# A gated linear attention followed by an MLP mixer: the mixer input of batch 0 made transposed in PSUM, channel weights loaded in three-chunk pieces, all orders rewritten

## The chip, the cores and the metric

The kernel runs on one core of a Trainium2 chip. The metric is the device time in microseconds (us) of one execution; shorter is better. Five engines work side by side and meet at semaphores: TensorE (PE: matrix products into PSUM), VectorE (DVE), ScalarE (ACT), GpSimd (POOL) and SyncE (SP, which issues most of the DMA transfers). Each engine takes its instructions strictly in the order in which the program lists them, apart from weight loads (PEld), which run ahead of the products.

## The reference

For each of 4 batches, 8 heads and 768 positions a 48x48 state is decayed, updated and read; the eight heads' outputs side by side make a row `x` of 384 values per position, and these go through a token mixer and a channel mixer:

```python
for t in range(S):                                  # S = 768
    state = alpha[:, :, t, :, None] * state + k[:, :, t, :, None] * v[:, :, t, None, :]
    y[:, :, t] = einsum('bhd,bhde->bhe', q[:, :, t], state)
x = y.transpose(0, 2, 1, 3).reshape(4, 768, 384)
h  = relu(x.transpose(0, 2, 1) @ w_tok1) @ w_tok2   # w_tok1 768x256, w_tok2 256x768
u  = x + h.transpose(0, 2, 1)
out = u + relu(u @ w_ch1) @ w_ch2                   # w_ch1 384x1536, w_ch2 1536x384
```

Inputs and output are float32 in HBM; the products are made in bfloat16.

## The kernel before, in words

The attention is worked in 12 chunks `n` = 0 to 11, three per batch, each of 256 positions held as 128 partitions by 2 slots. Every chunk has four loads of 384 KB (`ld_at` alpha, `ld_kt` k, `ld_qt` q, `ld_vt` v). ACT takes logarithms (`ln`), PE sums them along the positions with a triangular matrix (`cum`), ACT makes the decay factors (`E`, `IE`), DVE or POOL multiply them into q and k (`qq`, `kk`, line 700), both are transposed (`trq`, `trk` on PE at line 712 and `evq`, `evk` out of PSUM; for `n` from 6 on by DMA, `dq`, `dk`, line 725), PE makes the position-by-position products (`G`) that DVE masks (`mask`, line 770), PE makes the state update (`K`), DVE adds and scales it (`sa`, `sm`, `s`), and PE makes the output from the masked products (`y`) and from the state before (`ia`, `ib`). `x` copies it out of PSUM. Many small products share the helper of line 643.

The mixer of batch `b` follows. `t1` (line 878) and the relu `ht` are the first token product. `t2` (line 883) is the second, one 128-position tile `i` at a time, with its result laid out positions by channels; `u` (line 887, DVE) adds `x`. The channel product needs `u` transposed. For batches 1 to 3 a DMA does that (`ux`, line 729, one for each half of the positions); for batch 0 PE transposes (`up`, line 894, 18 products of 128 columns in three groups) and `ut` copies the result out of PSUM. `c1` (line 902, 24 blocks of three 384-column products per batch) and the relu `rt` (lines 873 and 875, on ACT or DVE) are the first channel product; `c2` (line 907, four blocks per tile) and `o` (line 911, DVE, which adds `u`) the second; `st` stores (line 624).

The weights come through the same 19 input buffers as the attention inputs: `ldw` loads a piece of 384 KB, `cw` casts it to bfloat16. `wc1` (w_ch1) has six pieces, each one 128-row chunk by 768 columns, so that the first `c1` block waits for three pieces; `wt2` has two pieces of 128 rows.

Nothing is scheduled when the kernel runs. A planner was run beforehand, and its answer is written into the file: `ORDER` lists all operations with a letter for the engine (`t` PE, `s` ACT, `v` DVE, `g` POOL, `y` SP), and each engine follows it; `BUFS` says which buffer each value takes. `f8_cumw1` and the like are filler products on zeros ahead of an operation on PE: the number counts units, three of which make one float32 product (line 643, `128*64 128x384 f32`) and the rest bfloat16 products of 512 columns.

Of the kernel before, what the change touches and what calls it, by code (L numbers as in the profile page):

```python
# [56 lines left out]
def either(*ds):  # L57
    out = {}
    for d in ds:
        out.update(d)  # L60
    return out
# [40 lines left out]
UP = (0,)  # L102
# [18 lines left out]
def build(g):  # L121

    P = Plan()
# [6 lines left out]
    def fillers():  # L130
        for o in list(P.ops):
            nm = o.name
            if "PE" in o.eng and (nm[:4] in ("t1_0", "t2_0", "up_0") or nm.split("_")[-1][-1] in "0123" and nm[:2] not in ("t1", "t2", "up", "c1", "c2") and not nm.endswith("10") and not nm.endswith("11")):
# [182 lines left out]
    def mixer(b):  # L316
# [15 lines left out]
        us = []  # L332
        for i in range(NS):
            if i % 3 == 0:
                u = V("u")
            bank = V("one")
            o = P.op(f"t2_{b}_{i}", pe([384] * 2), m0 + (1900 + 330 * i) * sc, writes=[bank],
                     reads=[h for h, _ in hts], preds=[h for _, h in hts] + [wl[("wt2", p)] for p in range(2)],
                     emit=lambda e, i=i, bank=bank: g.tok2(bank, i, [h for h, _ in hts]))
            uo = P.op(f"u_{b}_{i}", dve(384), m0 + (1950 + 330 * i) * sc, writes=[u], reads=[bank, x[i][0]], preds=[o],  # L340
                      emit=lambda e, i=i, bank=bank, u=u: g.uadd(u, i, bank, x[i][0]))
            us.append((u, uo))
        ut = V("ut")
        uts = []
        if b in UP:
            for p in range(3):
                bank = V("one")
                o = P.op(f"up_{b}_{p}", pe([128] * 6), m0 + (3900 + 340 * p) * sc, writes=[bank],
                         reads=list(dict.fromkeys([us[2 * p][0], us[2 * p + 1][0]])),
                         preds=[us[2 * p][1], us[2 * p + 1][1]],  # L350
                         emit=lambda e, p=p, bank=bank: g.utr(bank, [us[2 * p][0], us[2 * p + 1][0]], p))
                uts.append(P.op(f"ut_{b}_{p}", either(dve(768, True), act(768)), m0 + (3950 + 340 * p) * sc, writes=[ut],
                                reads=[bank], preds=[o], emit=lambda e, p=p, bank=bank: g.utev(e, ut, bank, p)))
        else:
# [18 lines left out]
        for i in range(NS):  # L373
            hold = 4000.0 if (i >= NS - 3 and b < B - 1) else 0.0
            cuts = [(0, HD // 2), (HD // 2, HD)] if (b, i) == LAST else [(0, HD)]
            for ci, (ca, cz) in enumerate(cuts):
# [33 lines left out]
ld_at1y ld_at0y ln1s ln0s f8_cumw1t f1_cumw1t cumw1t IE1s cumw0t IE0s ld_vt0y E0s vb0g vs0_0g vs1_0v ld_kt0y kk0v  # L410
f8_trk0t f1_trk0t trk0t E1s ld_qt0y qq0v ka0s kb0s kc0v f1_trq0t trq0t ld_kt1y kk1v K0t evq0s s0_0v ld_vt1y vb1s
f1_trk1t trk1t ld_at2y evk0v ln2s f2_G0_0t G0_0t ld_qt1y ka1g sa1_0v f4_cumw2t cumw2t mask0_0v vs0_1s kb1g kc1g vs1_1s
K1t sm1_0g qq1v sa0_1v sm0_1v G1_0t ld_kt2y IE2s E2s trq1t evq1s ib0t mask1_0v f3_y1_0t y1_0t y0_0t evk1v G0_1t sa1_1v
ld_qt2y x1_0s mask0_1v G1_1t ld_vt2y x0_0s vb2s kk2g trk2t kc2s ldw_wt10y qq2g cw_wt10s f2_ia1t ia1t mask1_1v evk2s
trq2t ld_at3y vs1_2g ldw_wt11y evq2v ib1t y1_1t y0_1t vs0_2g ldw_wt21y sm1_1g P3g K2t sa0_2v sm0_2g x0_1s t1_0_0_0t
f1_G0_2t G0_2t ldw_wt20y G1_2t cw_wt20g t1_0_1_0t mask0_2v x1_1s t1_0_1_1t ld_at4y ld_kt3y t1_0_1_2t lnP3s cum3t
cw_wt11s IE3s ia2t y0_2t x0_2s t1_0_0_1t t1_0_0_2t E3s t1_0_0_3t mask1_2v t1_0_1_3t ib2t y1_2t ldw_wc14y t1_0_1_4t
x1_2s t1_0_0_4t f1_t1_0_1_5t t1_0_1_5t ht_0_1v P4g cw_wt21s t1_0_0_5t ht_0_0s f3_t2_0_0t t2_0_0t t2_0_1t u_0_0v ln13s
r13s ldw_wc13y t2_0_2t u_0_1v t2_0_3t u_0_2v t2_0_5t lnP4s t2_0_4t u_0_3v u_0_5v u_0_4v up_0_0t cw_wc14s cw_wc13s
ldw_wc15y up_0_1t ld_qt3y k0a3g kk3g cum4t trk3t cw_wc15g ut_0_0v up_0_2t ut_0_2v ut_0_1s c1_0_11_0t c1_0_8_0t IE4s  # L420
c1_0_11_1t rt_0_8_0v rt_0_11_0v ldw_wc11y q0r3g qq3g c1_0_9_1t rt_0_9_1v ln14s kb3s c1_0_10_0t cw_wc11s c1_0_9_0t
rt_0_9_0v rt_0_11_1v E4s c1_0_7_0t c1_0_10_1t c1_0_7_1t ldw_wc10y r14s cw_wc10s rt_0_10_1v trq3t evk3s rt_0_7_0v
ldw_wc12y ld_vt3y cw_wc12g c1_0_2_0t c1_0_0_1t ka3g rt_0_7_1s c1_0_8_1t rt_0_10_0v vb3v vs1_3g vs0_3g rt_0_0_1v
rt_0_2_0v evq3s ld_at5y ld_qt4y c1_0_1_1t rt_0_8_1v c1_0_3_0t kc3s K3t P5g c1_0_4_1t rt_0_3_0s rt_0_1_1s q0r4g G0_3t
ld_kt4y qq4g s0_3v ln15s G1_3t sa1_3v c1_0_2_1t rt_0_2_1s mask0_3v lnP5s c1_0_1_0t c1_0_5_1t rt_0_5_1s rt_0_1_0s r15s
mask1_3v ldw_wc21y cw_wc21s k0a4g ldw_wc20y c1_0_6_1t rt_0_6_1v c1_0_4_0t kk4v ldw_wc22y c1_0_5_0t c1_0_0_0t cw_wc22s
rt_0_4_0v rt_0_0_0v cw_wc20g rt_0_4_1s c1_0_6_0t rt_0_6_0v c1_0_3_1t trq4t rt_0_3_1v cum5t trk4t ld_kt5y k0a5g
ldw_wc23y rt_0_5_0s c2_0_3_0t c2_0_5_0t evq4s kb4s evk4v ld_qt5y G1_4t mask1_4v G0_4t ld_vt4y c2_0_0_0t IE5s c2_0_0_1t
ka4g cw_wc23s c2_0_3_1t kc4s sm1_3g E5s mask0_4v ib3t y1_3t ldw_wc24y cw_wc24s c2_0_5_1t vb4g vs1_4s x1_3s ia4t
ldw_wc25y vs0_4g cw_wc25s ld_at6y y0_3t kk5v c2_0_3_2t y0_4t q0r5v trk5t evk5s qq5v K4t c2_0_0_2t sa0_4v c2_0_0_3t P6v  # L430
x0_3s ld_at7y sm0_4g o_0_0v trq5t x0_4s sa1_4v P7g evq5s lnP6s c2_0_5_2t c2_0_5_3t ld_vt5y vb5g c2_0_4_0t c2_0_4_1t
ld_kt7y kc5g G1_5t G0_5t lnP7s o_0_5v ib4t y1_4t vs1_5s mask1_5v t1_1_1_0t t1_1_1_1t sm1_4g x1_4s c2_0_4_2t c2_0_3_3t
vs0_5s ld_at8y t1_1_1_2t st_0_5s K5t mask0_5v sa0_5v sm0_5v cum6t t1_1_0_0t ld_kt6y k0a6g t1_1_0_1t ld_qt6y c2_0_2_0t
ln17s ld_qt7y ia5t y0_5t x0_5s IE6s kk6g ib5t y1_5t ln16s E6s t1_1_0_2t x1_5v t1_1_0_3t t1_1_1_3t cum7t E7s o_0_3v
t1_1_1_4t t1_1_1_5t r16s ld_kt8y q0r6g ld_vt6y dk6y P8g ht_1_1v lnP8s t1_1_0_4t t1_1_0_5t c2_0_2_1t c2_0_2_2t ln18s
ht_1_0v t2_1_1t u_1_1v t2_1_2t t2_1_0t t2_1_4t u_1_2v u_1_0v ux_1_0y c2_0_1_0t c2_0_1_1t vb6s IE7s qq6v r17s t2_1_3t
# [529 lines left out]
```

## Time and profile before

| | before |
|---|---|
| time, median of 3 runs (lowest to highest) | 163.17 us (162.33 to 164.11) |
| span of the profiled execution | 160.5 us |
| median less span (launch and end, outside the span) | 2.67 us |
| PE busy | 154.6 us |
| DVE busy | 114.9 us |
| ACT busy | 97.8 us |
| POOL busy | 80.8 us |
| HBM read and written | 25.17 MB and 4.72 MB |

The profile is one execution. Its busy PE is modelled: products overlap one another, so that the distance from one start to the next, not the length of one, says how long a product keeps PE.

### The profile page before, as it was taken

The page shows a single profiled execution, that of the slowest core. Times are in us where ns is not written, and L with a number is a line of the kernel's source. Part 1 is how long each engine was busy: PE and PEld are TensorE (multiplying, and loading weights), DVE is VectorE, ACT ScalarE, POOL GpSimd, SP SyncE. Part 2 cuts the span into 40 slices and gives each one's busy share as a digit, 9 for nine tenths or more (in the row PEclk, how much of TensorE's full clock was granted, in tenths as well). Part 3 has the DMA queues.
Part 4 walks back from the last instruction along what each step waited for, and adds up shares of the span by engine and source line. Part 5 has one row for each costly group of instructions (what it writes and reads, how often), then busy time and mean ns, then how long its engine had stood idle before and what let it go on. Part 6 is the DMA issues. An engine that isn't in the chain of part 4 may idle for free.

```text
span 160.5 us, 3971 instructions
## 1 busy us (share of the span) xinstructions
PE 154.6 (96%) x1563; PEld 97.1 (60%) x1563; DVE 114.9 (72%) x206; ACT 97.8 (61%) x179; POOL 80.8 (50%) x94
## 2 busy tenths in 40 slices
PE   7999989999999999999999999999999999999992
PEld 2545565766667676666667666566567665665661
DVE  6099994979889787989969758795886762464222
ACT  3789999998899955897563583269832203343000
POOL 5205897695973649389778852699523000000000
PEclk9999999999999999999999999999999999999999
DMA  4999999999999999999989999989701235111133
GB/s 122 320 324 317 317 374 311 339 333 306 316 347 324 275 278 272 210 228 319 241 202 298 239 315 204 217 196 134 196 21 62 87 79 169 49 49 53 49 129 116
DMA packets 76130, 35.05 MB, mean 218 GB/s; under 512 B 70352, under 2 KB 74320, under 8 KB 76112
## 3 DMA queue, kind: packets, MB, share of 16 engines
q1 hardware_dynamic: 73808, 31.76, 74.1%
q10 hardware_dynamic: 2304, 3.05, 5.3%
q8 instruction: 12, 0.20, 0.5%
q14 instruction: 6, 0.05, 0.1%
HBM read 25.17 MB, written 4.72 MB: 186 GB/s over the span
## 4 chain that ended last, share of the span: by engine, by line
PE 61%; DMA 12%; DVE 6%; ACT 6%; SPq 6%; POOL 4%; issue 3%; DVEq 0%; POOLq 0%
PE ps L907 22%; PE ps L902 21%; PE ps L643 11%; DMA in<-in_v_dram 6%; SPq L584 6%; DMA out_dram<-o 4%; PE ps L878 3%; PE ps L883 2%; DMA ut<-u 2%; DVE pkk L700 2%; DVE gtm L770 1%; PE ps L712 1%; DVE rt L875 1%; POOL vb L746 1%; POOL pkq L700 1%
## 5 line engine op out<-in xcount | busy, mean ns | idle before, releaser
L907 PE MATMUL ps<-wc,rt 128*128 128x384 bf16 (+1 forms) x300 | 52.4, 319 | 0.0
L902 PE MATMUL ps<-ut,wc 128*128 128x384 bf16 x288 | 50.3, 326 | 0.1
L902 PEld LDWEIGHTS <-wc 128*128 128x128 bf16 x288 | 27.1, 98 | 17.9 <-DMA ut<-u 0.6
L907 PEld LDWEIGHTS <-rt 128*128 128x128 bf16 x300 | 27.8, 98 | 16.0
L873 ACT ACTIVATE rt<-ps 128x384 bf16<-128x384 f32 x47 | 21.4, 492 | 23.6 <-PE ps L902 23.3
L875 DVE TENSOR_SCALAR rt<-ps 128x384 bf16<-128x384 f32 x49 | 25.6, 551 | 9.1 <-PE ps L902 8.9
L770 DVE TENSOR_TENSOR gtm<-ps,mk 128x1024 bf16<-128x1024 f32 x24 | 28.5, 1218 | 3.1 <-PE ps L643 2.8
L911 DVE TENSOR_TENSOR o<-ps,u 128x384 f32<-128x384 f32 (+1 forms) x25 | 13.2, 536 | 12.6 <-PE ps L907 10.1
L700 POOL TENSOR_TENSOR pkk<-in,IE 128x768 bf16<-128x768 f32 x8 | 14.5, 1817 | 3.3 <-DVE ss L844 2.3
L745 ACT CAST x<-ps 128x384 bf16<-128x384 f32 x20 | 9.2, 479 | 11.1 <-PE ps L643 9.5
L887 DVE TENSOR_TENSOR u<-ps,x 128x384 bf16<-128x384 f32 x24 | 12.0, 550 | 3.1 <-PE ps L883 2.5
L746 POOL CAST vb<-in 64x384 bf16<-64x384 f32 (+1 forms) x14 | 8.3, 594 | 10.4 <-DMA in<-in_v_dram 4.7
L692 POOL TENSOR_TENSOR in<-in,in 128x384 f32<-128x384 f32 x8 | 8.0, 1000 | 10.5 <-DVE u L887 3.8
L643 PE MATMUL ps<-rt 128*128 128x512 bf16 (+1 forms) x29 | 12.1, 515 | 1.1 <-DVE rt L541 1.1
L745 ACT CAST vb<-in 64x384 bf16<-64x384 f32 (+1 forms) x18 | 11.4, 634 | 0.8 <-DMA in<-in_v_dram 0.3
L700 POOL TENSOR_TENSOR pkq<-in,E 128x768 bf16<-128x768 f32 x6 | 10.9, 1818 | 0.6 <-DMA tpk<-pkq 0.3
L878 PE MATMUL ps<-x,wt 128*128 128x384 bf16 x48 | 11.0, 325 | 0.0
L844 POOL TENSOR_TENSOR ss<-tmp,E 128x384 bf16<-128x384 f32 x10 | 8.3, 833 | 4.2 <-DVE in L628 3.9
L841 DVE TENSOR_TENSOR tmp<-ps,ss 128x384 f32<-128x384 f32 x16 | 8.8, 552 | 1.8 <-PE ps L643 0.6
L883 PE MATMUL ps<-ht,wt 128*128 128x384 bf16 x48 | 9.1, 326 | 0.0
L643 PE MATMUL ps<-vb,gtm 128*128 128x48 bf16 x192 | 8.2, 183 | 0.2 <-DVE gtm L770 0.2
L643 PE MATMUL ps<-tpq,tpk 48*64 48x128 bf16 (+1 forms) x288 | 7.9, 218 | 0.4 <-POOL tpq L746 0.3
(94 smaller groups left out, 207.6 us busy)
## 6 DMA issues: line engine op xcount, KB each, us to landing
in<-in_alpha_dram SPq DMA_DIRECT2D x12, 384.0 KB, 5.1
in<-in_v_dram SPq DMA_DIRECT2D x12, 384.0 KB, 5.6
in<-in_k_dram SPq DMA_DIRECT2D x12, 384.0 KB, 5.2
in<-in_q_dram SPq DMA_DIRECT2D x12, 384.0 KB, 5.5
in<-in_moe_w_ch_dram SPq DMA_DIRECT2D x12, 384.0 KB, 5.9
out_dram<-o ACTq DMA_DIRECT2D x15, 192.0 KB, 1.8
in<-in_moe_w_tok_dram SPq DMA_DIRECT2D x4, 384.0 KB, 6.0
out_dram<-o SPq DMA_DIRECT2D x8, 192.0 KB, 2.2
```

The source lines that it names most:

```text
L643: return self.pe.matmul(out, lhsT=lhsT, rhs=rhs, start=start, stop=stop, skip_group_check=True)
L700: self.shared(self.eng[e].tensor_tensor(self.t(dst)[:, :, h0:h1, 0:D], self.t(src)[:, h0:h1].rearrange("p h s d -> p s h d"), bass.AP(tens ...
L745: return self.act.copy(d, s)
L770: self.nc.vector.tensor_tensor(self.t(gtm)[:, hf, :, :], self.pair(gp).rearrange("p a (j t) -> p (a j) t", t=128), bass.AP(tensor=m.tensor ...
L873: self.act.activation(d, s, AF.Relu)
L875: self.nc.vector.tensor_scalar_max(d, s, 0.0)
L878: self.pe.matmul(self.bank(bank)[:, 0:HD], lhsT=self.wt1[:, kc, m * 128 : m * 128 + 128], rhs=self.t(x), start=(kc == 0), stop=(kc == NS - 1))
L883: self.pe.matmul(self.bank(bank)[:, 0:HD], lhsT=self.wt2[:, kc, i * 128 : i * 128 + 128], rhs=self.t(hts[kc]), start=(kc == 0), stop=(kc = ...
L887: self.nc.vector.tensor_tensor(self.t(u)[:, i % 3], self.bank(bank)[:, 0:HD], self.t(x), ALU.add)
L902: self.pe.matmul(self.bank(bank)[:, 0:HD], lhsT=self.wc1[:, kc, mc * 128 : mc * 128 + 128], rhs=self.t(ut)[:, 3 * half : 3 * half + 3, kc, ...
L907: self.pe.matmul(self.bank(bank)[:, 0 : cz - ca], lhsT=self.t(rts[mc][0])[:, i * 128 : i * 128 + 128], rhs=self.wc2[:, mc, ca:cz], start=( ...
L911: self.nc.vector.tensor_tensor(self.t(o)[:, ca:cz], self.bank(bank)[:, 0 : cz - ca], self.t(u)[:, i % 3, ca:cz], ALU.add)
```

## The change

For batch 0 there is no `t2`, `u`, `up` any more. For each half of the positions and each of three 128-channel chunks `j`, PE first puts `x` transposed into a bank (`xa`: three products of 128 columns, with an identity matrix as the moving operand) and then adds the token product with the operands the other way round (`tt`: two products of 384 columns). The bank then holds a third of one half of `u` transposed, and `ut` copies it out on ACT or DVE, six copies of 384 columns. As `u` itself isn't there any more, the residual of the output is added in PSUM: the first `c2` block of each of the six tiles of batch 0 has three more products of 128 columns, of `ut` with the identity (`resid`), and `o` of batch 0 becomes a copy that ACT or DVE can do.

`wc1` is loaded as six pieces of 256 columns with all three row chunks, so that a piece serves two of the twelve column blocks by itself, and `wt2` as two pieces that serve one half of the positions each. `ORDER` and `BUFS` are new for the whole kernel, on all engines and queues; the filler blocks ahead of operations go from 13 with 36 units to 8 with 28.

```diff
-UP = (0,)
+UP = ()
+UDIR = (0,)
...
+        if b in UDIR:
+            ut, us, uts = V("ut"), [], []
+            for half in range(2):
+                evs = []
+                if half in (0, 1):
+                    for j in range(NM):
+                        bank = V("one")
+                        tx = x[3 * half : 3 * half + 3]
+                        xa = P.op(f"xa_{b}_{half}_{j}", pe([128] * 3), m0 + (1700 + 900 * half + 60 * j) * sc, writes=[bank],
+                                  reads=[v for v, _ in tx], preds=[o for _, o in tx],
+                                  emit=lambda e, bank=bank, tx=tx, j=j: g.xadd(bank, [v for v, _ in tx], j))
+                        o = P.op(f"tt_{b}_{half}_{j}", pe([384] * 2), m0 + (1900 + 900 * half + 330 * j) * sc, writes=[bank],
+                                 reads=[h for h, _ in hts], preds=[h for _, h in hts] + [xa, wl[("wt2", half)]],
+                                 emit=lambda e, bank=bank, half=half, j=j: g.tok2t(bank, half, j, [h for h, _ in hts]))
+                        evs.append(P.op(f"ut_{b}_{half}_{j}", either(act(384), dve(384)), m0 + (1950 + 900 * half + 330 * j) * sc,
+                                        writes=[ut], reads=[bank], preds=[o],
+                                        emit=lambda e, bank=bank, half=half, j=j: g.utev3(e, ut, bank, half, j)))
+                    uts.append(evs)
+                    us += [(ut, evs)] * 3
...
-                         reads=[ut], preds=(uts[0:2 + half] if b in UP else [uts[half]]) + [wl[("wc1", p)] for p in ((0, 1, 2) if mc < 6 else (3, 4, 5))],
+                         reads=[ut], preds=(uts[half] if b in UDIR else uts[0:2 + half] if b in UP else [uts[half]]) + [wl[("wc1", mc // 2)]],
...
+                    ri = q4 == 0 and b in UDIR and i // 3 in (0, 1)
+                    prev = P.op(f"c2_{nm}_{q4}", pe([cz - ca] * 3 + [128] * 3 * ri), m0 + (16700 + 1950 * i + 487 * q4) * sc + hold,
...
+                ri = b in UDIR and i // 3 in (0, 1)
+                oo = P.op(f"o_{nm}", either(act(384), dve(384)) if ri else dve(cz - ca), m0 + (16750 + 1950 * (i + 1)) * sc + hold, writes=[o_],
...
+    def xadd(self, bank, xs, j):
+        for i, x in enumerate(xs):
+            self.mm(self.bank(bank)[:, i * 128 : i * 128 + 128], self.t(x)[:, j * 128 : j * 128 + 128], self.idn, i == 0, False)
+
+    def tok2t(self, bank, half, j, hts):
+        for kc in range(NDT):
+            self.mm(self.bank(bank)[:, 0:HD], self.t(hts[kc])[:, j * 128 : j * 128 + 128],
+                    self.wt2[:, half, kc, :], False, kc == NDT - 1)
+
+    def utev3(self, e, ut, bank, half, j):
+        self.copy(e, self.t(ut)[:, 3 * half : 3 * half + 3, j, :], self.bank(bank)[:, 0:HD].rearrange("p (i t) -> p i t", i=3))
+
+    def resid(self, bank, ut, i):
+        for j in range(NM):
+            self.mm(self.bank(bank)[:, j * 128 : j * 128 + 128], self.t(ut)[:, i, j, :], self.idn, False, False)
```

The new `ORDER` from its start to the first channel blocks:

```
ld_kt1y ld_at0y ln0s f12_cumw0t f2_cumw0t cumw0t ld_at1y ln1s E0s IE0s cumw1t IE1s ld_qt0y qq0v f2_trq0t trq0t E1s
ld_kt0y kk0v trk0t ld_at2y ln2s f1_cumw2t cumw2t kk1v trk1t evq0s evk0v G0_0t ka0g ld_qt1y kc0v G1_0t qq1v trq1t evk1v
mask0_0v E2s mask1_0v IE2s ld_vt0y vb0g vs1_0s kb0s vs0_0g f4_K0t K0t s0_0v sa1_0v evq1s f3_G0_1t G0_1t ka1s kc1s
mask0_1v ld_qt2y qq2g G1_1t kb1s trq2t ld_vt1y vb1g vs0_1s y0_0t ib0t y1_0t ld_kt2y kk2g vs1_1s sm1_0g x0_0v mask1_1v
f2_K1t K1t trk2t ld_vt2y vb2g sa0_1v evk2v sm0_1g sa1_1v ia1t y0_1t ld_at3y P3g evq2s f2_G0_2t G0_2t mask0_2v ib1t
y1_1t ln13s x0_1s kc2s vs0_2s x1_0s K2t xa_0_0_0t sm1_1g sa0_2v lnP3s G1_2t mask1_2v x1_1s cum3t ia2t y0_2t xa_0_0_2t
ld_kt3y ldw_wt10y cw_wt10g t1_0_0_0t t1_0_0_1t t1_0_1_0t sm0_2g ib2t ldw_wt20y vs1_2s t1_0_1_1t y1_2t t1_0_0_2t
t1_0_1_2t IE3s cw_wt20s x0_2s x1_2s ldw_wt11y cw_wt11v t1_0_0_3t r13s t1_0_0_4t t1_0_1_3t t1_0_0_5t ht_0_0s xa_0_1_2t
t1_0_1_4t t1_0_1_5t ht_0_1s k0a3v kk3v trk3t xa_0_0_1t xa_0_1_0t ldw_wt21y cw_wt21v ld_qt3y q0r3v E3s tt_0_0_1t
xa_0_1_1t tt_0_1_0t ut_0_0_1s tt_0_0_0t tt_0_0_2t tt_0_1_2t qq3v tt_0_1_1t trq3t ut_0_0_2v ka3s ldw_wc15y cw_wc15g
ut_0_0_0s c1_0_11_0t evk3v ut_0_1_0v rt_0_11_0v c1_0_10_0t ldw_wc10y cw_wc10g ut_0_1_2s ut_0_1_1s c1_0_11_1t c1_0_0_1t
...
```

and the passage from batch 0 to the channel blocks of batch 1:

```
...
q0r6g ld_at7y P7g c2_0_4_1t c2_0_4_2t lnP8s st_0_2s ht_1_1v t2_1_0t u_1_0v ln17s IE6s t2_1_1t kk6g u_1_1v r17s t2_1_2t
r18s t2_1_5t t2_1_3t u_1_2v E6s st_0_0s u_1_5v u_1_3v t2_1_4t u_1_4v c2_0_1_0t ka6v c2_0_4_3t o_0_3s ld_qt7y q0r7g
c2_0_1_1t c2_0_1_2t c2_0_1_3t ld_vt6y vb6s st_0_5s vs1_6g lnP7s qq6g cum7t E7s o_0_4v st_0_4s cum8t IE8s kb6v o_0_1v
IE7s E8s ld_qt8y qq7v ux_1_0y c1_1_6_0t c1_1_0_0t c1_1_1_0t rt_1_0_0s c1_1_8_0t q0r8g c1_1_4_0t rt_1_4_0v rt_1_1_0s
...
```

More of the change, by code (lines that the diff above doesn't have):

```diff
@@ L331, in mixer @@
             hts.append((ht, ho))
[L332 to L342, printed above, removed]
@@ L415 @@
[L415 to L419, printed above, removed]
@@ L420 @@
[L420 to L424, printed above, removed]
@@ L613, in wcast @@
         elif nm == "wt2":
[L614 removed]
+            d, t = self.wt2[:, piece], t.rearrange("p (c m) -> p c m", c=2)
         elif nm == "wc1":
[L616 to L618 removed]
+            d = self.wc1[:, :, 256 * piece : 256 * piece + 256].rearrange("p c (r k) -> p c r k", r=2)
+            t = t.rearrange("p (c k r) -> p c r k", c=3, r=2)
         else:
```

177 lines of the change are left out of this document (90 added, 87 removed), and 22 rows, old and new, of the table BUFS.

## The prediction

> **What bounds the kernel now.** First the page: span, engines, clock, DMA. Then the stretches of the span, to see which engine is full where.
>
> ```profile
> span 160.5 us, 3971 instructions
> PE 154.6 (96%) x1563; PEld 97.1 (60%) x1563; DVE 114.9 (72%) x206; ACT 97.8 (61%) x179; POOL 80.8 (50%) x94
> PEclk9999999999999999999999999999999999999999
> ...
> 20.00:25.00 5.00, 4.53 (x78) 3.18 (x77) 4.88 (x6) 4.74 (x10) 4.25 (x7) 1.00 1.10 365
> ```
>
> PE is busy for 96% of the span, at full granted clock, but busy includes filler. Up to about 25 us another engine is full: in the row of 20 to 25 us (columns PE, weight loads, DVE, ACT, POOL) DVE works 4.88 of 5 us. So there are two regimes: DVE's queue feeds the attention of batch 0, and after that PE's own list. Where the second begins is read from PE in order of time.
>
> ```profile
> 26.94 0.86 PE L643 MATMUL ps<-rt 128*64 128x384 f32 x2
> 27.73 2.28 PE L883 MATMUL ps<-ht,wt 128*128 128x384 bf16 x12
> 29.85 0.83 PE L894 MATMUL ps<-idn,u 128*128 128x128 bf16 x12
> ...
> 30.81 0.61 PE L712 MATMUL ps<-idn,pkk 128*128 128x128 bf16 x8
> 31.25 0.50 PE L894 MATMUL ps<-idn,u 128*128 128x128 bf16 x6
> 31.76 4.55 PE L902 MATMUL ps<-ut,wc 128*128 128x384 bf16 x27
> ...
> 157.44 0.36 DVE L911 TENSOR_TENSOR o<-ps,u 128x192 f32<-128x192 f32 x1 [0.43 <-PE ps L907]
> ```
>
> Filler to 27.7, `t2` from 27.73, the transposes `up` from 29.85, the first `c1` at 31.76, and the last product just ahead of the last `o` at 157.44. From 31.76 on PE runs through 125.7 us. How much of that is waiting? I take start-to-start distances:
>
> ```profile
> 133.97 10.72 PE ps L902 x66
> ...
> 45.87 0.61 PE L712 MATMUL ps<-idn,pkk 128*128 128x128 bf16 x8
> 46.31 1.14 PE L907 MATMUL ps<-wc,rt 128*128 128x384 bf16 x6
> 47.40 0.62 PE L643 MATMUL ps<-tpq,tpk 48*128 48x128 bf16 x16
> 47.95 1.64 PE L907 MATMUL ps<-wc,rt 128*128 128x384 bf16 x9
> 49.43 0.33 PE L643 MATMUL ps<-ss,tpq 128*128 128x96 bf16 x4
> 49.60 0.36 PE L643 MATMUL ps<-vb,gtm 128*128 128x48 bf16 x8
> 49.80 0.65 PE L907 MATMUL ps<-wc,rt 128*128 128x384 bf16 x3
> ...
> 58.37 0.33 PE L643 MATMUL ps<-la,u 128*128 128x384 bf16 x1
> ...
> 58.66 0.48 PE L878 MATMUL ps<-x,wt 128*128 128x384 bf16 x2
> ...
> 73.11 0.64 PE L643 MATMUL ps<-tpq,tpk 48*64 48x128 bf16 x32
> 73.69 3.59 PE L902 MATMUL ps<-ut,wc 128*128 128x384 bf16 x21
> ```
>
> A 384-column product takes 10.72/66 = 0.1624 us; eight 128-column transposes 0.44 (0.055 each); the 16 products of `G` 0.55, in the 32-product form 0.58; four of `ia`/`ib` 0.17, and I give four of `K` the same; eight of `y` 0.20; one `cum` 0.29. Behind 31.76 stand 288 `c1`, 276 `c2`, 36 `t1` and 36 `t2` products: 636 x 0.1624 = 103.3 us. Twenty-four half-width `c2` at half of that add 2.0. The attention of chunks 3 to 11 adds 5 transposes (2.2), 7 `cum` (2.0), 60 products of `K` (2.55), `G` (3 x 0.55 + 6 x 0.58 = 5.1), 15 `ia`/`ib` (2.55) and 18 `y` (3.6). The sum is 123.3, so about 2.4 us are waits and rounding. Behind the first `c1` only PE work, and those 2.4, can be won or lost; ahead of it, the date on which `c1` can begin.
>
> **The change part by part.** The sum goes against the profiled execution: 160.5 us of span and whatever lies around it. That rest isn't in the trace; the median of the runs stands 2.67 us above the span, and I carry the change over to 163.17.
>
> *The date of the first `c1`.* The new DVE list up to `mask1_2` has four multiplies `qq`/`kk`, three `evk`, six masks, six adds or copies of 384 columns and one `kc`.
>
> ```profile
> 8.72 0.96 DVE L700 TENSOR_TENSOR pkk<-in,IE 128x768 bf16<-128x768 f32 x1
> 9.59 0.95 DVE L700 TENSOR_TENSOR pkq<-in,E 128x768 bf16<-128x768 f32 x1
> ...
> 12.21 0.68 DVE L746 COPY tpk<-ps 128x1024 bf16<-128x1024 bf16 x1
> ...
> 23.17 2.36 DVE L770 TENSOR_TENSOR gtm<-ps,mk 128x1024 bf16<-128x1024 f32 x2
> ...
> 28.27 2.88 DVE L887 TENSOR_TENSOR u<-ps,x 128x384 bf16<-128x384 f32 x6 [0.83 <-PE ps L883]
> ...
> 25.99 0.48 ACT L745 CAST x<-ps 128x384 bf16<-128x384 f32 x1
> ```
>
> 4 x 0.87 + 3 x 0.6 + 6 x 1.18 + 6 x 0.48 + 0.3 = 15.5 us. The list begins about 8.5 (its `E0` comes a little before the `IE0` on which the old list's 8.72 waited), and I find two small waits, for k of chunk 0 and for POOL's `sm0_1`, together 0.6: `mask1_2` ends near 24.8, where the old one ends at 23.17 + 2.36 = 25.5. Then `y1_2` and `x1_2`: to 26.1, where the old copy ends at 26.47. The second half of `t1` waits for a weight piece:
>
> ```profile
> 6.91 1.39 POOL L746 CAST vb<-in 128x768 bf16<-128x768 f32 x2 [4.11 <-DMA in<-in_v_dram]
> ...
> 24.76 0.82 POOL L746 CAST wt<-in 128x768 bf16<-128x768 f32 x1 [0.56 <-DMA in<-in_moe_w_tok_dram]
> ```
>
> The third load landed at 6.9 and the seventeenth at 24.7: 1.27 us per load, by SP's order. In the new list `wt11` is the seventeenth and `wt21` the eighteenth, so cast by DVE by 25.3 and 27.1; `t1` ends about 27.0 and `ht` 27.5. In this hole PE now does `trk3` and two `xa` instead of filler; `tt` starts about 27.8, as `t2` did. But then come only 12 x 0.1624 of `tt`, one `xa` (0.17) and `trq3` (0.44): 30.4. The eviction that `c1` needs last (`ut_0_0_2`, DVE, behind `qq3`) ends near 29.9, so PE's list decides. Against 31.76 that is **-1.35 us**: the 18 `up` products (1.0) and the round through `u` are gone. With no gain at all ahead of `mask1_2` it would be about 0, and if DVE's 0.6 of waits go too, -2. I keep both. `wc15` is the twentieth load (28.5, cast by POOL by 29.4), and one piece now serves four blocks, 1.95 us of PE against 1.27 per load, so `c1` stays fed.
>
> *What PE gets behind it.* `resid`: 18 products of 128 columns at 0.055 = **+1.0 us**. No row shows this product with `ut` as weights; the transposes at line 712 have its size and operand types, and at most it could cost 0.1624, which would make 2.9. `cum4` moves behind the first `c1` (+0.29), `trq3` ahead of it (-0.44): **-0.15**. `xa` (18 products, 1.0) lies ahead of `c1` and is in the date above.
>
> *What costs nothing.* Six `u` adds of 0.48 leave DVE, two eviction copies and one on ACT become six: both lists get shorter, and `o` of batch 0 may go to ACT; PE hides all of it, as long as banks come free. The wc1 pieces have rows of 1 KB, not 3 KB; attention loads with rows of 384 bytes keep the pace of 1.27 us, so the price is bounded by that pace and hidden behind `c1`. The end has the same shape: a half-width block, `o`, one store.
>
> *The new order elsewhere.* Sums of each engine's listed work between PE's stages stay below PE's in both orders, so I take the same 2.4 us of waits; zero to five is possible. **Sum: -1.35 + 1.0 - 0.15 = -0.5: 162.7 us.**
>
> **The clock.** One measured fact speaks against the change, which takes filler away.
>
> ```profile
> 1.06 4.21 PE L643 MATMUL ps<-rt 128*64 128x384 f32 x7 [1.06 <-DVE rt L541]
> ...
> 7.34 2.26 PE L643 MATMUL ps<-rt 128*64 128x384 f32 x7
> ```
>
> The first seven filler products took 4.21 us, the same seven later 2.26: 1.9 times, although the granted clock reads full. The new first block is shorter (four float32 products and two others, done by about 4.4) and leaves PE idle until `cumw0` at 6.4. If PE were slow again there, `cumw0` and `cumw1` would take 0.7 us longer in front of the DVE list: 163.4. The Trainium skill (TensorE: Matmul & The Clock Gate, Part 1) says that PE starts at half clock, is released after some 3.4 us of sustained work and falls back after an idle window as long; by its figure two idle microseconds are too short, and the sum stays as it is.
>
> **The rivals.**
>
> *More of the waits go.* Half of the 2.4 us of waits and another 0.5 ahead of `c1` (the DVE waits): 162.7 - 1.7 = 161.0. For it: DVE and ACT have less to do around the first `c1`. Against it: no wait in PE's list is longer than half a microsecond, so nothing large is left.
>
> *The start isn't shorter.* If loads or DVE's chain hold `mask1_2` at 25.5, `t1` and `c1` follow, the change only adds `resid`: 163.17 + 1.0 - 0.15 = 164.0. The full DVE row speaks for it.
>
> *A transpose DMA comes late (slower).* The place is `ux_1_0`, ahead of the first `c1` of batch 1.
>
> ```profile
> 103.65 0.42 SPq L584 DMA_DIRECT2D in<-in_q_dram  x1
> 104.16 1.87 SPq L725 DMA_TRANSPOSE tpk<-pkq  x1
> ...
> DMA to landing us min/median/max: 5.9/5.9/5.9
> ...
> DMA to landing us min/median/max: 2.8/3.0/3.8
> ```
>
> A transpose issued right behind a load landed after 5.9 us (third row); those of `u` take 2.8 to 3.8 (last row). In the new SP list `ux_1_0` stands right behind six loads, and what PE has behind `t2_1_2` is three `t2` (0.97), one `c2` block with `resid` (0.65), four without (1.95) and two `cum` (0.58): 4.15 us. `u_1_2` ends about 1.05 behind `t2_1_2`, so 3.0 just fits; above 3.1 PE stands still, and at 5.9 for 2.8 us: 165.5. If those loads are through by then it is free: their buffers were read long before, so SP can run ahead at 1.27 per load, the 49th being issued near 62 us (48 x 1.27 behind the first); PE's list, summed as above, puts the start of `t2` of batch 1 some 31 us behind the first `c1`, and `u_1_2` near 64. That is close.
>
> **How the numbers follow.** The three runs of before spread over 1.1%, so 1% (161.54 to 164.80) is about what can be told from no change. Forecast 162.7: 0.27. More waits go, 161.0: 0.27, faster. Start not shorter, 164.0: 0.15, of which 0.03 above 164.80. Late transpose, 165.5: 0.25, slower. Slow clock, 163.4: 0.06, of which 0.02 above. So faster 0.27, same 0.27 + 0.12 + 0.04 = 0.43, slower 0.30. The range starts 0.6 below the faster rival, at 160.4 (`c1` earlier by 2, half the waits gone), and ends at 166.4, 0.9 above the late transpose, for the upper bound of `resid`; outside lie fewer waits still, and a second late transpose.
>
> **What would show it.** PE in order of time: first `c1` at 30.4 (29.7 to 31.8), `tt` near 27.8; `resid` at 0.055 apiece; no idle PE ahead of line 902 near 67 us; `ux_1_0` landing in 3 us; last `o` near 157. It is wrong if PE shows waits of over a microsecond behind 32 us, in places that I didn't name.

## The result, and the profile after

Timed in turns, the kernel after takes **165.17 us** (median of 13 runs, 163.74 to 169.13) and the kernel before 163.09 (13 runs), a ratio of **1.0126, 95% interval 1.0095 to 1.0157**. It is slower by 1.3%, where 0.3% faster was forecast; the range of 160.4 to 166.4 holds it. The ratio leaves out executions that took over 1.5% more than the fastest of their kernel, four of the 13 after and one of the 13 before. The profiled execution took 165.17 us with a span of 163.5, 3.0 us longer than the span of before.

The page of after, its span and engine lines, then the granted clock and the stretch of 60 to 70 us:

```profile
span 163.5 us, 3995 instructions
PE 154.0 (94%) x1574; PEld 98.0 (60%) x1574; DVE 114.6 (70%) x203; ACT 96.9 (59%) x183; POOL 75.3 (46%) x90
PEclk9999999999999999999999999999999999999998
...
60.00:70.00 10.00, 9.46 (x92) 6.05 (x89) 6.27 (x13) 7.11 (x16) 7.21 (x8) 1.00 1.07 270
```

Against before, PE is busy 0.6 us less in a span 3.0 us longer, at full clock: PE now stands still. PE in order of time around the first channel block shows what happened to the date on which the forecast gain rested (line 737 is `trk3` and then `trq3`, line 943 `c1`):

```profile
27.44 0.49 PE L903 MATMUL ps<-x,wt 128*128 128x384 bf16 x2
28.14 0.62 PE L737 MATMUL ps<-idn,pkk 128*128 128x128 bf16 x8 [0.21 <-DVE pkk L725]
28.60 0.50 PE L668 MATMUL ps<-idn,x 128*128 128x128 bf16 x6
28.93 0.49 PE L668 MATMUL ps<-wt,ht 128*128 128x384 bf16 x2
29.26 0.33 PE L668 MATMUL ps<-idn,x 128*128 128x128 bf16 x3
29.43 1.79 PE L668 MATMUL ps<-wt,ht 128*128 128x384 bf16 x10
31.05 0.61 PE L737 MATMUL ps<-idn,pkq 128*128 128x128 bf16 x8
```

`tt` begins at 28.93, not near 27.8, and the first `c1` behind `trq3` at 31.52, not 30.4: 0.24 us ahead of before instead of 1.35. Behind it PE runs to the last `o` as before, but with three waits of a length that the trace of before does not have at all:

```profile
68.36 0.32 PE L668 MATMUL ps<-la,u 128*128 128x384 bf16 x1 [0.54 <-ACT la L659]
92.34 0.42 PE L668 MATMUL ps<-tpq,tpk 48*64 48x128 bf16 x16 [0.85 <-DVE tmp L866]
124.71 0.34 PE L668 MATMUL ps<-vb,pkk 128*128 128x96 bf16 x4 [0.97 <-DVE gtm L795]
```

From start to start PE loses 0.71, 0.98 and 1.13 us there, 2.8 together. The releasers named, `la`, `tmp` and `gtm`, are none of the changed operations. What made them late is read from ACT and DVE in order of time, together with the queue that issues the stores:

```profile
62.33 0.38 ACTq L649 DMA_DIRECT2D out_dram<-o  x1
66.67 0.48 ACT L770 COPY o<-ps 128x384 f32<-128x384 f32 x1 [1.17 <-DMA out_dram<-o]
67.78 0.52 ACT L659 ACTIVATE la<-in 128x384 bf16<-128x384 f32 x1
...
85.22 0.45 ACTq L649 DMA_DIRECT2D out_dram<-o  x1
89.66 0.56 DVE L952 TENSOR_TENSOR o<-ps,u 128x384 f32<-128x384 f32 x1 [0.93 <-DMA out_dram<-o]
91.73 0.55 DVE L866 TENSOR_TENSOR tmp<-ps,ss 128x384 f32<-128x384 f32 x1
...
118.66 0.34 ACTq L649 DMA_DIRECT2D out_dram<-o  x1
122.97 0.56 DVE L952 TENSOR_TENSOR o<-ps,u 128x384 f32<-128x384 f32 x1 [1.27 <-DMA out_dram<-o]
123.44 2.35 DVE L795 TENSOR_TENSOR gtm<-ps,mk 128x1024 bf16<-128x1024 f32 x2
```

Each time the same three steps. A store is issued late or lands slowly (62.33 to 66.7, 85.22 to 89.7, 118.66 to 123.0: 4.3 us each). The `o` that is to write its output buffer stands still at the head of ACT or DVE, since there are three buffers. Behind it in the same list stands something that PE needs: `lnP7` for `cum7`, the `sa`/`sm` chain ending in `sa0_8`, whose bank `G0_8` takes, and `mask1_11`, whose bank `K11` takes. The tile view of `o` sums it up, after first and then before (the line counts how long its engine sat idle for a store, and how often):

```profile
  DMA out_dram<-o: 6.1, 5
DMA to landing us min/median/max: 1.7/2.3/5.7
```

```profile
  DMA out_dram<-o: 2.5, 3
DMA to landing us min/median/max: 1.6/2.0/5.8
```

So before had such waits too, but none that reached PE: its longest idle there behind the first `c1` is 0.28 us, at 116.29, and not for a store. The 2.8 us of these waits and the -0.24 of the date, with the forecast's own +1.0 for `resid` and -0.15 for `cum4` and `trq3`, make 3.4 us for 3.0 of span; 0.4 is rounding or made up elsewhere.

### The profile page after: what moved, and what is told of

Read it like the earlier page. It is cut to its first block, busy times and chain, and to the rows that moved or that the text cites. A ratio compares the mean times of both kernels' runs of the same rounds, so it can differ in the third digit from the quotient of the medians.

```text
span 163.5 us, 3995 instructions
## 1 busy us (share of the span) xinstructions
PE 154.0 (94%) x1574; PEld 98.0 (60%) x1574; DVE 114.6 (70%) x203; ACT 96.9 (59%) x183; POOL 75.3 (46%) x90
## 4 chain that ended last, share of the span: by engine, by line
PE 55%; DMA 18%; DVE 14%; issue 4%; POOL 3%; ACT 2%; SPq 2%; ACTq 0%; DVEq 0%; POOLq 0%
PE ps L943 21%; PE ps L948 19%; PE ps L668 9%; DMA out_dram<-o 8%; DVE gtm L795 5%; DMA in<-in_moe_w_tok_dram 4%; DMA in<-in_k_dram 4%; PE ps L903 4%; DMA in<-in_alpha_dram 3%; DVE pkk L725 2%; PE ps L737 2%; DVE o L952 2%; PE ps L908 2%; DVE u L912 1%; POOL pkq L725 1%
## 5 line engine op out<-in xcount | busy, mean ns | idle before, releaser
L898 ACT ACTIVATE rt<-ps 128x384 bf16<-128x384 f32 x52 | 23.8, 492 | 26.7 <-PE ps L943 26.5
L900 DVE TENSOR_SCALAR rt<-ps 128x384 bf16<-128x384 f32 x44 | 22.9, 552 | 10.1 <-PE ps L943 9.6
L952 DVE TENSOR_TENSOR o<-ps,u 128x384 f32<-128x384 f32 (+1 forms) x19 | 9.9, 532 | 14.2 <-PE ps L948 10.0
L771 POOL CAST vb<-in 64x384 bf16<-64x384 f32 (+1 forms) x17 | 10.1, 597 | 10.1 <-ACT vb L770 3.3
L725 POOL TENSOR_TENSOR pkq<-in,E 128x768 bf16<-128x768 f32 x7 | 12.7, 1814 | 1.8 <-DMA tpk<-pkq 1.4
L668 PE MATMUL ps<-rt 128*64 128x384 f32 (+1 forms) x22 | 9.7, 555 | 1.1 <-DVE rt L564 1.1
L912 DVE TENSOR_TENSOR u<-ps,x 128x384 bf16<-128x384 f32 x18 | 8.9, 550 | 2.0 <-PE ps L908 2.0
L725 POOL TENSOR_TENSOR pkk<-in,IE 128x768 bf16<-128x768 f32 x5 | 9.1, 1815 | 0.9 <-ACT kt L770 0.7
L668 PEld LDWEIGHTS <-tpk 48*64 48x64 bf16 (+1 forms) x288 | 5.8, 102 | 5.4 <-issue 4.1
L771 POOL CAST wc<-in 128x768 bf16<-128x768 f32 x7 | 6.0, 864 | 6.5 <-DVE pkq L725 5.3
```

The costliest lines, as they stand in the source:

```text
L668: return self.pe.matmul(out, lhsT=lhsT, rhs=rhs, start=start, stop=stop, skip_group_check=True)
L725: self.shared(self.eng[e].tensor_tensor(self.t(dst)[:, :, h0:h1, 0:D], self.t(src)[:, h0:h1].rearrange("p h s d -> p s h d"), bass.AP(tens ...
L771: return self.shared(self.eng[e].tensor_copy(d, s))
L898: self.act.activation(d, s, AF.Relu)
L900: self.nc.vector.tensor_scalar_max(d, s, 0.0)
L912: self.nc.vector.tensor_tensor(self.t(u)[:, i % 3], self.bank(bank)[:, 0:HD], self.t(x), ALU.add)
```

## The experiments

Theory: the new order puts `o`s that wait for a store ahead of work that PE needs. Rivals: the new way through `tt` costs more on PE than thought, or the weight pieces do, or the transpose DMA of batch 1 is late.

**Six output buffers instead of three.** Twice: in the kernel after and, for control, in the kernel before. Three of the 20 `rt` buffers make room, and the values of both `o` and `rt` take their buffers in turn.

```diff
-    ... "rt": 20, "o": 3,
+    ... "rt": 17, "o": 6,
```

> The changed kernel with six output buffers for `o` instead of three, taken in turn (and 17 instead of 20 buffers for `rt`, in turn, to make room). Theory S (stores): the three long waits of PE behind 32 us (0.7 at 67.7, 1.0 at 91.4, 1.1 at 123.6) come from an `o` that stands in front of the work PE needs, waiting for a buffer whose store has not landed; with six buffers they go, about 2.5 us: near 162.9, a ratio to before of 1.00. Rival P (path): the loss is work on PE and the start; the waits on stores only move, and the time falls by less than 0.5: 164.8 or more, ratio 1.01.

Measured 162.77 against 162.85, ratio 0.9999 (0.9967 to 1.0032). All of the 1.3% is gone. No `o` waits for a store any more, and none of the three PE waits is there. Two of them are not replaced by anything; PE's only wait of over 0.2 us behind the first `c1` (at 30.86 here) is this one:

```profile
67.54 0.17 PE L672 MATMUL ps<-off,idn 128*128 128x16 bf16 x1
68.16 2.12 PE L947 MATMUL ps<-ut,wc 128*128 128x384 bf16 x12 [0.45 <-DMA ut<-u]
```

> The kernel before with the same six output buffers. Theory S: its `o` waits for stores three times too (2.5 us on DVE in all), but PE shows no wait behind them: no change, ratio 0.997 to 1.003. If PE's small waits there also come from stores, ratio 0.99.

The first control, 162.97 and 0.9979 (0.9940 to 1.0018), took the buffers strictly in turn; in the old order, where one store stands very late, tile 0 of batch 1 was then stored with another tile's data. So it was made again with the buffer that has been free longest:

> The kernel before with six output buffers instead of three, each time the one that has been free longest. Theory, none of the old order's waits for a store reaches PE, so more buffers change nothing: 163.1, ratio 1.000. Rival, output buffers hold the kernel before too, a little: 162.0 to 162.5, ratio 0.995.

162.34 against 162.77, 0.9986 (0.9951 to 1.0020). Buffers do nothing for the kernel before: the loss belongs to the new order.

**The three blocking `o`s moved back.**

```diff
-... c2_0_4_3t o_0_3s ld_qt7y ... cum7t E7s o_0_4v
+... c2_0_4_3t ld_qt7y ... cum7t E7s o_0_3s o_0_4v
-... x0_6v o_1_2v y0_7t ... sa0_8v o_1_3v
+... x0_6v y0_7t ... sa0_8v o_1_2v o_1_3v
-... o_2_4v sm1_10g ... mask1_11v G0_11t mask0_11v
+... sm1_10g ... mask1_11v G0_11t mask0_11v o_2_4v
```

> The changed kernel with its three output buffers, but with the three blocking o's moved back in their engine's list: o_0_3 behind lnP7 and E7 on ACT, o_1_2 behind sa0_8 on DVE, o_2_4 behind mask0_11 on DVE. Theory, the loss comes from what stands behind a blocked o in the engine's list: the three PE waits of 0.7 to 1.1 us at 67.6, 91.4 and 123.6 go, and the time falls by 2.2 to 2.8 us to 162.4 to 163.0, about equal to the kernel before. Rival, three buffers with late stores are too few wherever the o's stand: the waits come back at the next o or at a bank that isn't freed, and the time stays at 164.5 or above.

164.20, ratio 1.0089 (1.0060 to 1.0119), between the two. The interval overlaps that of the change itself (1.0095 to 1.0157), so it isn't shown that any of the loss went; most of it stayed, and by the rival's mechanism. PE in order of time:

```profile
68.44 0.32 PE L669 MATMUL ps<-la,u 128*128 128x384 bf16 x1 [0.96 <-ACT o L771]
92.47 0.64 PE L669 MATMUL ps<-tpq,tpk 48*64 48x128 bf16 x32 [1.54 <-DVE o L953]
125.13 0.33 PE L669 MATMUL ps<-ss,tpq 128*128 128x96 bf16 x4 [0.18 <-DVE o L953]
```

The third wait fell from 1.13 to 0.34, but in the first two PE now waits for the `o` itself, 1.12 and 1.70 us from start to start where it was 0.71 and 0.98: 3.2 in all, not less than the 2.8. (This span is 0.7 us shorter than that of the change; its first `c1` came at 30.91 instead of 31.52.) `cum8` takes the PSUM bank that `o_0_3` reads, `G1_8` that of `o_1_2`. Early, the `o` blocks its engine; late, it holds a bank.

**Earlier stores, with three buffers.** No `o` is moved.

```diff
-... o_0_2v ... o_0_0s ... o_0_5s ln18s ... st_0_2s ... st_0_0s ... st_0_5s
+... o_0_2v ... st_0_2s o_0_0s ... o_0_5s st_0_0s ln18s st_0_5s
-... st_0_4s ... rt_1_3_0s ... st_0_1s ... st_0_3s
+... st_0_4s st_0_3s ... rt_1_3_0s st_0_1s
     (output of tile 4 of batch 2: buffer 1 -> 0)
```

> The changed kernel with its three output buffers, but with the stores of tiles 2, 0, 5, 3 and 1 of batch 0 issued earlier in ACT's list (2 and 0 some 5 us, 5 some 7, 1 some 13 and 3 some 25 us earlier), and with the output of tile 4 of batch 2 in buffer 0 instead of 1, whose store is older. No o is moved. Theory, the late landing of the stores is what blocks the o's: the three PE waits of 0.7 to 1.1 us go without another buffer, 162.6 to 163.2, ratio 0.998 to 1.003. Rival, three buffers are too few whenever the stores are issued, since a store takes 4 us or more among loads: 164.3 or above, ratio 1.009 or more.

162.86 against 162.50, ratio 1.0031 (0.9997 to 1.0066): the upper edge of the theory, below the rival's 1.009. The profiled execution took 165.86 us, 3 us above this median, so only the waits of `o` are read from it: one is left, ahead of an `o` at 139.08 (2.02 us), with nothing behind it that PE lacks. The longest idle of PE in that execution, 1.22 us at 92.13, is for a transpose DMA: on POOL `kc8` waited 2.36 us for `dk8`, and `sm0_7` stands behind it. So an earlier issue of the stores takes away most of the loss, perhaps all, without another buffer. It also settles a doubt about the six buffers, which came with a new use of the `rt` buffers: here those are as in the change.

**Without the residual products.** The output of batch 0 lacks its residual.

```diff
-(g.ch2(bank, i, q4, rts, ca, cz), g.resid(bank, ut, i) if ri else None)
+g.ch2(bank, i, q4, rts, ca, cz)
```

> The changed kernel without the 18 residual products of batch 0 (its output lacks that residual). Both theories: PE is full behind 32 us, so the 18 products at 0.055 cost 1.0 us: 164.2, ratio 1.006. If they lie in waits, nothing: 165.2, ratio 1.013.

166.43 against 162.85, ratio 1.0191 (1.0136 to 1.0246): with 1 us of work less, no gain at all. The profile is of an execution of 169.62 us, 3.2 above this median, so it shows what can happen, not what happens each time. In it PE reaches the waits earlier and waits longer; the second wait is for `ux_1_0`, issued at 63.73 and landed 6.2 us later. The same PE places, and the stretches of the span (the third number from the end is the granted clock):

```profile
67.50 0.32 PE L668 MATMUL ps<-la,u 128*128 128x384 bf16 x1 [1.26 <-ACT la L659]
69.98 2.27 PE L943 MATMUL ps<-ut,wc 128*128 128x384 bf16 x7 [1.75 <-DMA ut<-u]
```

```profile
60.00:70.00 10.00, 6.99 (x53) 4.13 (x51) 5.23 (x12) 6.64 (x16) 7.11 (x6) 1.00 1.12 261
70.00:80.00 10.00, 10.00 (x52) 5.59 (x53) 4.99 (x9) 5.14 (x12) 4.43 (x4) 0.83 1.04 255
```

PE is busy 6.99 of 10 us, and in the next 10 us the granted clock is 0.83. That is a mean: in windows of half a microsecond the clock reads 0.50 from 70.2 to 73.6 and 1.00 ahead of that and behind it, which costs 1.7 us of PE's work. A second such stretch, from 97.5 to 100.9, follows idle times of 0.39 and 1.55 us, and the two together make 3.4 us, about what this execution took above the median. The two of the six executions whose mean clock was 0.997 or more took 165.27 and 165.69, still no gain. So the price of `resid` can't be read from this run. With six buffers it should show:

> The changed kernel with six output buffers and without the 18 residual products, so that the output of batch 0 lacks its residual. Theory, with the output-buffer waits gone PE's own list decides: the 18 products of 0.055 us are worth 1.0 us, and against six buffers alone (162.8) the time falls to 161.8, ratio to the kernel before 0.994. Rival, as without the products and with three buffers, where nothing was gained: waits take the place of the products, or the granted clock falls, and the time is 162.8 or more.

162.65 against 162.77, ratio 0.9978 (0.9954 to 1.0001): against six buffers alone 0.2%, or 0.3 us, nearer the rival and not clear of the noise (the intervals overlap). PE shows where the rest went:

```profile
66.90 0.17 PE L672 MATMUL ps<-off,idn 128*128 128x16 bf16 x1
68.33 1.96 PE L947 MATMUL ps<-ut,wc 128*128 128x384 bf16 x11 [1.26 <-DMA ut<-u]
```

From the first `c1` (31.07) to `cum8` (66.90) PE took 35.83 us, with the products 36.68 (30.86 to 67.54): 0.85 of the 1.0 is there. But `c1` of batch 1 begins at 68.33 here and at 68.16 there. It begins when `ux_1_0` lands, and the saving becomes a wait.

**The new weight pieces alone**, in the kernel before with its old order.

```diff
-wl[("wc1", p)] for p in ((0, 1, 2) if mc < 6 else (3, 4, 5))
+wl[("wc1", mc // 2)]
     (and the six loads and casts of w_ch1 as in the change)
```

> The kernel before with w_ch1 in three-chunk pieces of 256 columns alone, its order unchanged. The first channel block there waits for `ut`, not for a piece, and the loads keep their pace: no change, ratio 0.997 to 1.003. If rows of 1 KB slow the loads, the casts come later and PE waits: ratio 1.005 or more.

163.29, ratio 1.0014 (0.9983 to 1.0045): no change that can be told. A small price isn't excluded: in the profile, of an execution of 164.19, PE idles 1.24 us at 52.43 until ACT has cast a piece of channel weights whose load came late, a wait that the profile of before doesn't have.

**An earlier first `c1`**, on top of six buffers.

```diff
-... ld_kt3y ldw_wt10y ... ldw_wt20y ... ldw_wt11y cw_wt11v
+... ldw_wt11y ldw_wt10y ... ldw_wt20y ... ld_kt3y cw_wt11v
```

> The changed kernel with six output buffers, and the loads of wt11 and of k of chunk 3 (14th and 17th in SP's list) exchanged, with their buffers. Theory, wt11's landing sets t1, ht and the first c1: c1 begins some 0.5 us earlier, time 162.3, ratio 0.997. Rival, k of chunk 3 is then the late load, and kk3 and trk3 in front of the token products hold them as long: 162.8, ratio 1.000.

162.44, ratio 0.9986 (0.9959 to 1.0012), not to be told from six buffers alone. The first `c1` began at 30.78, 0.08 ahead of the profile with six buffers, and PE then waited longer for the same DMA:

```profile
67.45 0.17 PE L669 MATMUL ps<-off,idn 128*128 128x16 bf16 x1
68.39 1.80 PE L944 MATMUL ps<-ut,wc 128*128 128x384 bf16 x10 [0.77 <-DMA ut<-u]
```

**The transpose of batch 1 brought forward**, on top of six buffers. `ux_1_0` was issued at 64.47 and landed some 3.6 us later, with a load ahead of it in flight.

```diff
-... ld_qt8y qq7v ux_1_0y
+... qq7v ux_1_0y ld_qt8y
```

> The changed kernel with six output buffers, and in SP's list the load of q of chunk 8 moved behind the first transpose DMA of u of batch 1. Theory, the first channel block of batch 1 begins when that transpose lands (68.2 to 68.4 us with and without the residual products, 3.6 to 4.3 us behind its issue), and the load in flight stretches the landing: it falls to 2.8 to 3.0 us, PE's wait of 0.6 goes, and the time is 162.2, ratio 0.996. Rival, the other loads stretch it as much: still 162.8, or slower where q of chunk 8 is now the late one.

> The same without the 18 residual products, so that the output of batch 0 lacks its residual. Theory, the products are worth 1.0 us of PE, and without them only 0.3 was gained (162.65 against 162.8) because PE then waited 1.4 us for the transpose: with the transpose landing earlier most of the 1.0 shows, 161.4 to 161.6, ratio 0.992. Rival, PE's work ahead of that place isn't what sets the time: 162.2 or more, no faster than with the products.

Both slower: 165.37, ratio 1.0102 (1.0047 to 1.0157), and 163.17, 1.0057 (1.0026 to 1.0088). The first half of the theory holds; the profile with the products (PE, then the tile view of `ut`):

```profile
67.75 4.07 PE L944 MATMUL ps<-ut,wc 128*128 128x384 bf16 x24
72.33 0.97 PE L944 MATMUL ps<-ut,wc 128*128 128x384 bf16 x5 [0.51 <-DMA ut<-u]
```

```profile
DMA to landing us min/median/max: 2.8/2.9/5.7
```

`c1` of batch 1 begins at 67.75, right behind `cum8`. But the load now stands ahead of `ux_1_1`, which takes 5.7 us, and the second half of the blocks waits for it. The transposes of chunks 6 to 8 stand behind that in SP's list, and PE waits 1.14 us at 80.30 and 1.31 at 91.90.

**All together**: six buffers, both swaps of loads, the earlier stores.

> The changed kernel with six output buffers, the loads of wt11 and of k of chunk 3 exchanged, q of chunk 8 behind the transpose, and the earlier stores of batch 0, all together. Theory, the first c1 at 30.8 and no wait of over 0.3 us behind it: 161.6 to 162.0, ratio 0.993 to 0.995, faster than both kernels. Rival, one of the moved loads takes over: 162.4 or above, ratio 0.998 or more.

163.65, ratio 1.0088 (1.0053 to 1.0123): no wait ahead of `c1` of batch 1, but 1.36 us ahead of its second half, as in the run above.

**Both transposes ahead of every load.** A first try (three kernels) had `P11` ahead of the load that it works on, and took 169.25 to 169.84 us because the load then waited for `P11` and held SP's list until 87.65; it tells nothing of the question. Its expectation, and those of the mended try:

> The changed kernel with six output buffers, and with no load between the last loads of chunk 6 and both transpose DMAs of u of batch 1: q of chunk 8 takes the place of alpha of chunk 11 in SP's list, alpha of chunk 11 goes behind v of chunk 8, and the POOL operations that read them move behind k0a7 and P9. Theory, both transposes land in 2.8 to 3.0 us (the second took 5.7 to 7.2 with the load between the two), c1 of batch 1 begins at 67.8 instead of 68.2 and nothing stands still behind it: 162.3, ratio 0.996. Rival, the moved loads make chunk 8 or 11 late: a PE wait of 0.5 us or more between 72 and 95, 163 or above.

```diff
-... ld_qt8y qq7v ux_1_0y ... q0r8g ... ux_1_1y ld_kt7y ... ld_at11y ... k0a7g ... P11g ... ld_vt8y ... vs0_8g
+... qq7v ux_1_0y ... ux_1_1y ld_kt7y ... ld_qt8y ... k0a7g q0r8g ... ld_vt8y ld_at11y ... vs0_8g P11g
```

> The same edit as in the first try with both transposes ahead of every load, with the one fault of that try mended (P11 stood ahead of the load of alpha of chunk 11 that it works on, so that it worked on old data, and the load waited for it and held SP's list until 87.65 us). Theory, as there: transposes of batch 1 land in 2.8 to 3.0 us, c1 of batch 1 at 67.7 to 67.8, no wait above 0.3 us behind it: 162.3, ratio 0.996. Rival, one of the moved loads (q of chunk 8, alpha of chunk 11) is late: a PE wait of 0.5 us or more between 72 and 95, 163 or above.

> The same without the 18 residual products, so that the output of batch 0 lacks its residual. Theory, at least half of the products' 1.0 us shows: 161.4 to 161.8, ratio 0.991 to 0.994. Rival, what stands ahead of the transpose doesn't set the time: as with the products.

> As the first, with the loads of wt11 and of k of chunk 3 exchanged too. Theory, 0.1 to 0.4 us less than the first by the date of the first c1: 161.9 to 162.2, ratio 0.993 to 0.996, faster than both kernels. Rival, the earlier date is swallowed at the transpose: as the first.

167.29, ratio 1.0281 (1.0220 to 1.0342); 164.13, 1.0113 (1.0070 to 1.0156); 166.72, 1.0205 (1.0161 to 1.0249). The transposes did land as expected and `c1` of batch 1 began at 67.76. The rival decided, 20 us later (first with the products, tile view of `ut`, PE, DVE, stretches):

```profile
DMA to landing us min/median/max: 2.8/2.8/3.3
```

```profile
67.76 2.45 PE L944 MATMUL ps<-ut,wc 128*128 128x384 bf16 x14
89.81 0.33 PE L669 MATMUL ps<-ss,tpq 128*128 128x96 bf16 x4 [0.71 <-POOL ss L870]
92.98 0.64 PE L669 MATMUL ps<-tpq,tpk 48*64 48x128 bf16 x16 [1.44 <-DVE tmp L867]
```

```profile
91.43 0.56 DVE L870 TENSOR_TENSOR ss<-tmp,E 128x384 bf16<-128x384 f32 x1 [1.08 <-POOL in L654]
```

```profile
80.00:90.00 10.00, 9.29 (x149) 6.14 (x148) 7.28 (x10) 7.66 (x13) 5.58 (x10) 1.00 1.17 280
90.00:100.00 10.00, 8.53 (x107) 5.35 (x104) 6.38 (x11) 3.20 (x8) 6.38 (x7) 0.83 0.85 234
```

The load of alpha of chunk 11, now behind v of chunk 8, stands ahead of the transposes of chunk 8. `dk8` landed late, `kc8` on POOL waited for it, and `sm0_7` behind that came late (the first wait). The run with `ux_1_0` brought forward and the profile of the earlier stores show the same wait, at 91.90 and 92.13, without this move, so that the moved load isn't shown to be its only cause. `P11` on POOL, moved, held DVE's `sm1_7` for 1.08 us. After 2.4 us of waits, from start to start, the granted clock is again 0.83 in the mean, 0.50 from 92.9 to 96.3. So a free transpose wins 0.4 us at 68 us, and each way that was tried to free it lost more behind it: these kernels take 0.6 to 2.8% longer than the kernel before, where six buffers alone take as long. Of the two runs without `resid`, one came out 2.2 and one 3.2 us below its partner. With these waits in between that is no measure of the products, and in the second pair the clock differs too: a mean of 0.998 or more in five of the six executions without `resid`, in one of the six with it. No version was found that beats both kernels: the best medians, 162.34 to 162.86, are within the interval of no change.

## Why the prediction was wrong

**The step that failed is the term "the same 2.4 us of waits" under "The new order elsewhere".** It was given zero to five; measured, it is some 2.8 us more, 5.2 in all. It was argued from sums of each engine's work, and the runs don't contradict these sums: with the store waits out of the way the same order runs as fast as the old one, and PE has one wait of over 0.2 us behind the first `c1`. What sums can't show is a wait for a resource that no engine's work contains, here an output buffer until its store has landed. The prediction let `o` of batch 0 go to ACT at no cost ("What costs nothing"), "as long as banks come free", and never asked when the output buffers come free. The first of the three waits has such an `o` on ACT at its head; the other two have an `o` of batches 1 and 2 on DVE, which the change leaves as it was but for its place in the list. A row of before that was not quoted had the answer's price: `o` sat 2.5 us for stores, three times.

**The date of the first `c1`** was to gain 1.35 and gained 0.24 in the profile of after; in ten other profiles of the new order, some with two loads exchanged, the first `c1` came at 30.8 to 31.1, which is 0.65 to 1.0 (in two more at 31.9 and 32.0). The mechanism was right, the size was off. DVE of the kernel after in order of time:

```profile
24.25 1.22 DVE L795 TENSOR_TENSOR gtm<-ps,mk 128x1024 bf16<-128x1024 f32 x1
25.99 0.56 DVE L771 CAST wt<-in 128x768 bf16<-128x768 f32 x1 [0.52 <-DMA in<-in_moe_w_tok_dram]
```

`mask1_2` ended at 25.47, not 24.8, so the gain ahead of it was nothing, and the cast of `wt11` waited for its load and began at 25.99, against "by 25.3" for its end, with `k0a3`, `kk3`, `trk3` behind it on DVE and PE. "The start isn't shorter" was that rival, at 164.0; it was half right, and too small alone. It took the gain for "about 0" once `mask1_2` ends at 25.5, but the prediction's own sum leaves half of it then: 0.7 of the 1.35 hangs on `mask1_2`, and the other 0.65 is what the slower of the ten profiles show. (Its DVE terms, 8.5 + 15.5 + 0.6, also make 24.6 and not 24.8.)

**`resid`** at 0.055 us apiece was right. PE of the kernel after:

```profile
46.10 0.33 PE L668 MATMUL ps<-idn,ut 128*128 128x128 bf16 x3
46.27 0.65 PE L948 MATMUL ps<-wc,rt 128*128 128x384 bf16 x3
```

Three take 0.17 us from start to start, and of the 1.0 for all 18, 0.85 showed in PE's stretch without them. **The pieces** at nothing are not contradicted (1.0014, at most 1.0045). **The clock at the start**: the rival of slow first products didn't occur, and its premise was off. The new first block of filler, 14 units instead of 9, is longer and not shorter, and PE is busy with it until `cumw0` at 6.38, not 4.4. The granted clock is full until 162 us, behind the last product.

**The late transpose** was placed rightly, at `ux_1_0`, and priced too high for most executions. In the profile of after and in those with six buffers and SP's old list around it, it lands in 3.4 to 4.3 us, not 5.9; in the profile without `resid` and with three buffers it took 6.2, so the rival's landing does occur. In the profile of after PE is later than it, because of `lnP7`, and it costs nothing: that this rival's 165.5 lies next to the 165.17 measured is luck. With six buffers it is what PE waits for, 0.6 to 1.4 us. That is where the rest of the forecast gain goes: `c1` of batch 1 began at 68.16, 68.39 and 68.33 with the first `c1` at 30.86, 30.78 and 31.07 and with or without `resid`. In these three profiles what was saved ahead of it ended in that wait: the transpose was issued at 64.47, 64.39 and 64.00 and landed 3.6, 4.0 and 4.3 us later, no sooner for an earlier issue. The runs meant to show that a saving gets through once the transpose is free lost more elsewhere, so this half, that it then reaches the end, stays argued and not shown.

The prediction named as its own falsification "waits of over a microsecond behind 32 us, in places that I didn't name", and waits in three places that it didn't name are what came, of 0.71, 0.98 and 1.13 us, so only one of them over a microsecond.

## What to carry to other kernels

When the order of an in-order engine changes, list for every operation that writes a buffer when the last reader of that buffer is done, the store's landing included, and what stands behind the operation on its engine; sums of work say nothing about it. Such a wait is paid at the engine's head or, if the operation is moved back, in the bank that it holds, so cure it at its source: issue the store earlier, which took the ratio to the kernel before from 1.0126 to 1.0031 here, or add a buffer. And before counting a saving, find the next date that doesn't move with it, here, in three profiles, the landing of a transpose. Where a mean clock falls short of 1, look at it in short windows.

## What the runs showed of the hardware

A store of 192 KB landed 1.8 to 1.9 us after its issue in the last 13 us of the kernel after, where no load was in flight, and 4.2 to 4.4 us after it in the three places among loads, and so decides when its buffer is free. The Trainium skill (DMA: Bandwidth & Descriptors, Anatomy of one DMA) gives, for transfers issued by GpSimd, a fixed 2.0 us plus the bytes at 436 GB/s; carried over to these stores, which ACT and SP issue, that makes 2.4, an estimate. The quiet landing here is shorter, the one among loads 1.8 to 2.0 us longer.

The transpose DMA of `u` landed in 2.8 us at the least, in 3.4 to 4.3 where the last load had been issued some 5 us earlier, once in 6.2 where it had been issued 3.5 us earlier, and in 5.7 to 7.2 behind a load that was issued 0.7 us earlier.

Idle times on PE of 1.26 and 1.75 us, 2.5 us apart, were followed by 3.4 us at a granted clock of 0.50, and so were 0.71 and 1.44, 3 us apart, and 0.39 and 1.55, 2 us apart. Single idle times of up to 1.54 us, and 1.15 with 0.47 behind it, left the clock full in 10 us around them. The Trainium skill (TensorE: Matmul & The Clock Gate, Part 1) speaks of a fall to half clock after an idle window of some 3.4 us. The half and the 3.4 us agree with these traces, but no single idle was that long: in the 3.4 us ahead of the three falls PE still had work for an estimated 0.8, 1.3 and 1.5 us, summed from the starts of its products. What decides between these cases and those without a fall stays open.
